# Splitting the memory-row hand-over and interleaving the Q and K passes in a recurrent memory transformer layer

## The chip, the cores and the metric

The kernel runs on one core of a Trainium2 chip. The metric is the device time of one execution in microseconds (us). Before the change, three runs took 2334.03, 2334.85 and 2330.82 us; their median is 2334.03 us. One more execution was profiled; its span from the first to the last instruction is 2335.8 us, at a mean granted TensorE clock of 0.98.

## The reference

Four layers in the order A, B, A, B work on `x` of 2048 tokens by 640 channels, each as `x = x + layer(layernorm(x))`. Layer A is a linear-memory attention over four segments; the change does not touch it. Layer B is recurrent over 64 segments of 32 tokens. Eight memory rows go in front of each segment, 32 heads of 128 channels attend over these 40 rows, and the output's first eight rows are the memory of the next segment:

```python
for s in range(n_seg):                       # 64
    xs = x[:, s * seg_len:(s + 1) * seg_len, :].copy()
    h = jnp.concatenate([mem, xs], axis=1)   # 8 + 32 rows
    q = jnp.einsum('btd,dhe->bhte', h, Wq)   # k and v likewise
    ...
    scores = jnp.where(mask[None, None], scores, -1000000000.0)
    p = _softmax(scores, axis=-1)
    o = jnp.einsum('bhqk,bhke->bhqe', p, v)
    o = jnp.einsum('bhte,hed->btd', o, Wo)
    mem = o[:, :M, :].copy()
    outs.append(o[:, M:, :])
```

A step can therefore not begin its projections of the memory rows before the output projection of the step before is complete.

## The kernel before, in words

**Order.** Every call on an engine goes through a recorder (line 85), which ties each instruction to the one before it on the same engine. So each engine's queue is the program order of the Python text, and nearly every instruction of the profile bears line 85; tiles (b_Qa, b_hT and so on) tell them apart. Waits between engines come from what reads and writes which tile.

**Layer B's step.** `layer_B` (line 661) runs 64 steps `s`; four of them make a tile `T` of 128 tokens, and `i4 = s % 4`. The stationary operand of a step, `hT[s]`, holds 5 chunks of 128 channels by 56 columns: 24 of the segment's own tokens, the 8 memory rows (columns 24 to 32), and 24 tokens of the next segment. The tokens are put there by GpSimd copies (`alloc_h`, line 729) one step ahead. A Q or K pass takes columns 24 to 56, so it computes the memory rows of this step and the tokens of the next; a V pass takes columns 0 to 32. The last 8 tokens of each segment, the tail, go another way: `tail_cols(T)` (line 776) gathers the tails of the four segments of a tile into `b_hx` on GpSimd, and `TailUnit`s project them for a whole tile at once.

**A pass.** `thin_parts` (line 750) makes five parts, one per chunk. Each part issues four matmuls into the four 32-partition strips of one PSUM tile (128x512 fp32). 32 heads need two passes each for Q, K and V; half b covers heads 16b to 16b+15. When a Q or K pass has run its last part (`QKPass.run`, line 1002), VectorE turns it by 32x32 blocks (`turn`, line 762, the STREAM_TRANSPOSE that writes b_TQ, two buffers), VectorE casts the memory rows into `QT[s]` or `KT[s]`, and GpSimd casts the other 24 columns into the tiles of step s+1 (`place`, line 768). When a V pass has ended, ScalarE (half 0) or VectorE (half 1) casts it into `b_Vsb`. The passes, the scores and the tail units take their PSUM tiles in turn from one pool of three (line 673).

**The order within a step** (lines 1097 to 1164): Q half 0, K half 0, Q half 1, two chunks of K half 1, scores of half 0, the other three chunks, V half 0 with the softmax sums of half 0 in it, scores of half 1, three chunks of V half 1, values of half 0, two chunks of V half 1, sums of half 1. `scores` (line 1022) begins with four mask matmuls that need neither Q nor K. Two ScalarE casts (`take`, line 1080) move the values of half 0 out of PSUM (b_OTL to b_OTsb). Then follow eight passes of two heads of the output projection (b_OPS), the values of half 1, and the last eight. `normalise` (line 1057) computes the inverse sums on ScalarE and multiplies b_PT on VectorE and on GpSimd.

**The hand-over.** After the output projection, VectorE turns all of b_OPS (128x320) into `b_TM` (line 1159), and two additions (line 1161) put the memory rows of all five chunks into `hT[s + 1]`. Meanwhile TensorE has filler: `fill` (line 956) takes from a queue of parts by written costs, about 0.44 us before the values of half 1, 0.66 us after them, and the rest behind the output projection. In steps with i4 of 1, 2 and 3 the queue holds the two tail units of V, Q or K of the next tile; in i4 = 0 it holds the deferred output projection of the tails of the last tile (b_OPSd). The last tile of a layer has no tail units. `flush` (line 822) finishes tail units whose parts are done: ScalarE casts V, VectorE turns Q and K and GpSimd casts them. Output rows are added to the residual on VectorE (b_XO, b_XOd): at once in steps with i4 = 1, in the middle of the next step otherwise.

Of the kernel before, what the change touches and what calls it, by code (L numbers as in the profile page):

```python
# [21 lines left out]
ALU = mybir.AluOpType  # L22
# [7 lines left out]
NCH = 5  # L30
# [630 lines left out]
def layer_B(nc, nc_raw, tc, C, W, br, outer, wo_src, x_src, xb_src, x_dst, general, nsteps=64, out_bf16=False):  # L661
# [3 lines left out]
    NT = nsteps // 4  # L665
    with ExitStack() as ctx:
# [34 lines left out]
        def ln_norm(g):  # L701
            xt = ln_x.pop(g)
            ln_n[g] = xt, layernorm_stats(nc, sm, C, xt[:], "b_ln")

        def ln_apply(g):
            xt, (mv, rstd) = ln_n[g]
            xn = ln_n[g] = wk.tile([128, D], BF16, name="b_xn", tag="xn")
            layernorm_apply(nc, xt[:], xn[:], mv, rstd)

        def ln_tr(g):  # L710
            xn = ln_n.pop(g)
            tps = pot.tile([128, NCH, 128], BF16, name="b_lntps", tag="ot")
            for c in range(NCH):
                nc.tensor.transpose(tps[:, c, :], xn[:, 128 * c:128 * c + 128], C.identb[:])
            xg = wk2.tile([128, NCH, 128], BF16, name="b_xnTg")
            nc.scalar.copy(xg[:], tps[:])
            xnT_g[g] = xg
# [6 lines left out]
        hT, QT, KT = {}, {}, {}  # L724
# [51 lines left out]
        def tail_cols(T):  # L776
            if T not in hx:
                hx[T] = wk.tile([128, NCH, 32], BF16, name="b_hx", tag="hx")
                v = xnT_g[T][:].rearrange("p c (i t) -> p c i t", t=32)[:, :, :, 24:32]
                nc.gpsimd.tensor_copy(hx[T][:].rearrange("p c (i t) -> p c i t", t=8), v)  # L780
            return lambda c: hx[T][:, c, :]
# [151 lines left out]
        for s in range(nsteps):  # L933
            last = (s == nsteps - 1)
            T, i4 = divmod(s, 4)
# [20 lines left out]
            def fill(us):  # L956

                while queue and us > 0.1:
                    cost, f = queue.pop(0)
                    f()  # L960
                    us -= cost
# [56 lines left out]
            def qk(Wt, name, b, dst):  # L1018

                QKPass(Wt, name, b, dst).run()  # L1020
# [27 lines left out]
            def sums(b):  # L1048

                sm_ = SP[b][:, 256:416].rearrange("p (r c) -> p r c", c=40)  # L1050
                for k in range(2):
                    for j in range(4):
                        nc.tensor.matmul(sm_[32 * j:32 * j + 32, :, 24 * k:40], lhsT=C.blk[:, j],
                                         rhs=PT[:, b, :, 0:16] if k else PT[:, b, :, 16:56], start=(k == 0), stop=(k == 1),
                                         tile_position=(0, 32 * j), skip_group_check=True)

            def normalise(b):

                R = (wk if general else sm).tile([128, 4, 40], F32, name="b_R", tag="R")
                flat = R[:].rearrange("p r c -> p (r c)")  # L1060
                nc.scalar.activation(out=flat, in_=SP[b][:, 256:416], func=ACT.Ln)
                nc.scalar.activation(out=flat, in_=flat, func=ACT.Exp, scale=-1.0)
                nc.vector.tensor_tensor(out=PT[:, b, :, 16:56], in0=PT[:, b, :, 16:56], in1=R[:], op=ALU.mult)
                nc.gpsimd.tensor_tensor(out=PT[:, b, :, 0:16], in0=PT[:, b, :, 0:16], in1=R[:, :, 24:40], op=ALU.mult)
                if not general:
                    nc.gpsimd.tensor_tensor(out=Rtot[:], in0=Rtot[:], in1=R[:], op=ALU.add)

            def values(b):
                for jp in range(2):
                    OTL[b, jp] = pair_tile("b_OTL")  # L1070
                for r in range(4):
                    for k in range(2):
                        V_ = Vtb[T] if k else Vsb
                        for j in range(4):
                            o = OTL[b, j // 2][:, j % 2, 40 * r + 24 * k:40 * r + 40]
                            nc.tensor.matmul(o, lhsT=V_[32 * j:32 * j + 32, b, 128 * r:128 * r + 128],
                                             rhs=PT[32 * j:32 * j + 32, b, r, 0:16] if k else PT[32 * j:32 * j + 32, b, r, 16:56],
                                             start=(k == 0), stop=(k == 1), tile_position=(32 * j, 0))

            def take(eng, b, jp):  # L1080
                h = 16 * b + 8 * jp
                evac(eng, OTsb[:, h:h + 8, :].rearrange("p (j r) c -> p j (r c)", j=2), OTL[b, jp][:, :, 0:160])
# [11 lines left out]
                    if not self.parts:  # L1094
                        evac(("act", "dve")[self.b], Vsb[:, self.b, :], self.ps[:])

            qk(W.wq, "b_Qa", 0, QT)
            qk(W.wk, "b_Ka", 0, KT)
            qk(W.wq, "b_Qb", 1, QT)
            if general:  # L1100
                row_max(0)
# [3 lines left out]
            K1.run(3)  # L1105
            while xn_pending:
                ln_tr(xn_pending.pop(0))
            if i4 == 0 and T + 1 < NT:
                tail_cols(T + 1)
            V0 = VPass(0)  # L1110
            V0.run(1)
            sums(0)
# [7 lines left out]
                nc.sync.dma_start(XO[32 * jj2:32 * jj2 + 24, :], x_src[32 * s:32 * s + 24, 320 * jj2:320 * jj2 + 320])  # L1120
            scores(1)
            V1 = VPass(1)
            V1.run(3)
            values(0)
            g_need = (s + 6) // 4 if s % 4 == 2 else NT
            if g_need < NT:
                ln_norm(g_need)
            V1.run(2)
            sums(1)
            take("act", 0, 0)  # L1130
            take("act", 0, 1)
            normalise(1)
            if g_need < NT:
                ln_apply(g_need)
                xn_pending.append(g_need)
            if i4 != 3:
                tails_to_seg(s + 1)
            op = OPass(lambda h: OTsb[:, h, 0:32], HORDER, "b_OPS", po, "op")
# [9 lines left out]
            ops = op.ps  # L1148
# [7 lines left out]
                deferred[T] = OPass(lambda h, t_=OTd: t_[:, h, :], HORDER, "b_OPSd")  # L1156
            if not last:
                TM = wk.tile([128, 10, 32], F32, name="b_TM", tag="TM")
                nc.vector.transpose(out=TM[:].rearrange("p g t -> p (g t)"), in_=ops[:])
                for hf in range(2):  # L1160
                    nc.vector.tensor_tensor(out=hT[s + 1][64 * hf:64 * hf + 64, :, 24:32], in0=TM[0:64, hf:10:2, 24:32],
                                            in1=TM[64:128, hf:10:2, 24:32], op=ALU.add)
            fill(9)
            flush()
            if not last and i4 == 3:
# [36 lines left out]
def full_kernel(tc, A_x, A_wq, A_wk, A_wv, A_wo, A_beta, B_x, B_mem0, B_Wq, B_Wk, B_Wv, B_Wo, B_seg_len, out, layers="ABAB"):  # L1202
    nc = tc.nc
    with ExitStack() as ctx:
# [14 lines left out]
        def run(general):  # L1219
            nc.scalar.preload_act_table_set("natural_log_exp_and_others")  # L1220
            nl = len(layers)
            assert layers == "AB" * (nl // 2)
            onc = _OrdNC(tc, nc, engines=ORDER_ENGINES)
            for li in range(0, nl, 2):
                lastl = (li == nl - 2)
                first = li == 0 and not general
                with ExitStack() as bridge, ExitStack() as outer:
                    outer.bridge = bridge
                    br = layer_A(onc, nc, tc, C, WA, A_wv, A_wo, xin if li == 0 else X, X, Xb, li == 0, general, outer, mem0,
                                 prep=prep if first else None, prefetch=loads if first else ())  # L1230
                    layer_B(onc, nc, tc, C, WB, br, outer, wo_src, X, Xb, xout if lastl else X, general, out_bf16=lastl)
# [61 lines left out]
```

## Time and profile before

| view | what it shows |
|---|---|
| span | 2335.8 us |
| busy, us | TensorE matmul 2225.5, VectorE 1576.3, GpSimd 1036.7, ScalarE 950.3 |
| layer B, typical step by i4 = 0, 1, 2, 3 | 12.92, 12.96, 13.06, 13.48 us from Q's first matmul to the next |
| VectorE, turning b_OPS | 126 times 517 ns |
| VectorE, additions into b_hT | 252 times 223 ns in the mean, 197 in the median |
| VectorE, turning a Q or K pass | 717 ns each |
| GpSimd, copy of tail columns into b_hx | 30 times 401 ns |

Busy time is the union of an engine's instruction times. Matmuls overlap, and their ends are modelled, so starts say more of TensorE than ends: the four matmuls of a chunk start within some 10 ns and the next four 216 ns after. In a list of waits, each row says which engine was idle, what ended that idle time, the total, how often and the longest. PEld is the loading of stationary operands, which runs ahead of the matmuls. In a timeline, each row has the start and the length in us, then the instructions merged into it; the bracket gives the idle time before and what ended it. POOL is GpSimd, DVE is VectorE, ACT is ScalarE.

### The profile page before, as it was taken

What the parts mean: (1) busy time and instruction counts of PE and PEld (TensorE: products, weight loads), DVE (VectorE), ACT (ScalarE), POOL (GpSimd) and SP (SyncE); (2) the same over time, 40 slices, a digit from 0 to 9 for tenths busy, and PEclk for the clock granted to TensorE, in tenths of its full rate; (3) what the DMA queues carried; (4) which work ended last, traced back from release to release, by engine and by line L of the source; (5) the groups of instructions that cost most, each with busy time, mean ns of one, the idle gap of its engine ahead of it and who ended that gap; (6) DMA issues with size and microseconds to landing.
All of it is one profiled execution on the core that took longest, in us unless ns stands there. A gap on an engine that the chain in (4) does not pass through costs nothing.

```text
span 2335.8 us, 122651 instructions
## 1 busy us (share of the span) xinstructions
PE 2225.5 (95%) x54988; PEld 1238.1 (53%) x54988; DVE 1576.3 (67%) x3618; ACT 950.3 (41%) x2207; POOL 1036.7 (44%) x2475
## 2 busy tenths in 40 slices
PE   6999989999999999999889899899999999999997
PEld 3444545555555555555545445455555555555554
DVE  5777746666666666666657777566666666666664
ACT  5776823323232333323257767223333233323332
POOL 3344534444444444444324445344444444444442
PEclk9999989999999999999989999999999999999998
DMA  6555540000000000000133334300000000000000
GB/s 165 146 148 152 161 142 20 21 18 20 18 19 19 20 21 20 21 15 17 31 104 115 108 117 127 124 18 15 17 15 17 16 18 16 17 18 16 14 12 14
DMA packets 90649, 123.38 MB, mean 53 GB/s; under 512 B 16496, under 2 KB 80000, under 8 KB 88192
## 3 DMA queue, kind: packets, MB, share of 16 engines
q1 hardware_dynamic: 87648, 111.84, 16.9%
q8 instruction: 431, 7.06, 1.3%
q10 hardware_dynamic: 2464, 3.61, 0.6%
q14 instruction: 106, 0.87, 0.1%
HBM read 89.17 MB, written 26.21 MB: 49 GB/s over the span
## 4 chain that ended last, share of the span: by engine, by line
PE 80%; DVE 10%; ACT 5%; issue 2%; DMA 2%; POOL 0%; SPq 0%; DVEq 0%; ACTq 0%; POOLq 0%
PE b_OPS L85 14%; PE b_V L85 13%; PE b_Qa L85 7%; PE b_tail L85 7%; PE b_Kb L85 6%; PE b_Ka L85 6%; PE b_Qb L85 6%; PE b_SP L85 4%; PE a_PP L85 4%; ACT a_PT L85 4%; PE b_OTL L85 3%; PE b_OPSd L85 3%; PE a_S L85 2%; PE a_pv L85 2%; DVE a_qk L85 2%
## 5 line engine op out<-in xcount | busy, mean ns | idle before, releaser
L85 PEld LDWEIGHTS <-b_hT 128*32 128x32 bf16 x15120 | 369.8, 96 | 334.7 <-DVE b_hT L85 66.6
L85 ACT ACTIVATE b_PT<-b_SP 128x224 bf16<-128x224 f32 x256 | 92.2, 360 | 784.6 <-DVE b_TQ L85 740.2
L85 PE MATMUL b_V<-b_wv,b_hT 128*32 128x512 bf16 x5040 | 355.8, 381 | 0.0
L85 ACT ACTIVATE a_PT<-a_S 128x768 bf16<-128x768 f32 (+1 forms) x384 | 326.7, 892 | 62.4 <-PE a_S L85 56.2
L85 PE MATMUL b_OPS<-b_wo,b_OTsb 128*32 128x320 bf16 x8192 | 329.9, 303 | 6.5 <-DVE b_OTsb L85 5.2
L85 PEld LDWEIGHTS <-b_OTsb 128*32 128x32 bf16 x8192 | 197.3, 97 | 115.4 <-DVE b_OTsb L85 49.4
L85 POOL CAST b_QT<-b_TQ 128x384 bf16<-128x384 f32 x254 | 142.7, 562 | 240.9 <-DVE b_TQ L85 240.9
L85 ACT CAST b_OTsb<-b_OTL 128x320 bf16<-128x320 f32 x384 | 151.0, 428 | 232.3 <-PE b_OTL L85 204.7
L85 POOL CAST b_KT<-b_TQ 128x384 bf16<-128x384 f32 x254 | 142.9, 563 | 175.5 <-DVE b_TQ L85 174.3
L85 POOL TENSOR_TENSOR b_PT<-b_PT,b_R 128x64 bf16<-128x64 bf16 x256 | 105.6, 412 | 222.1 <-ACT b_R L85 197.4
L85 POOL TENSOR_SCALAR_AFFINE_SELECT a_PT<-a_PT 128x256 bf16<-128x256 bf16 x256 | 109.0, 427 | 172.6 <-ACT a_PT L85 161.0
L85 PE MATMUL b_Kb<-b_wk,b_hT 128*32 128x512 bf16 x2520 | 182.5, 380 | 0.0
L85 PE MATMUL b_Qa<-b_wq,b_hT 128*32 128x512 bf16 x2520 | 162.3, 387 | 13.7 <-DVE b_hT L85 7.2
L85 PE MATMUL b_Ka<-b_wk,b_hT 128*32 128x512 bf16 x2520 | 160.0, 383 | 0.0
L85 PE MATMUL b_Qb<-b_wq,b_hT 128*32 128x512 bf16 x2520 | 158.1, 380 | 0.0
L85 PE MATMUL a_PP<-a_xnT,a_wt 128*128 128x512 bf16 x560 | 146.1, 394 | 5.2 <-DVE a_um L85 1.5
L85 DVE STREAM_TRANSPOSE b_TM<-b_OPS 128x320 f32<-128x320 f32 x126 | 65.1, 517 | 118.2 <-PE b_OPS L85 118.2
L85 PE MATMUL a_S<-a_qk 32*128 32x512 bf16 (+3 forms) x1024 | 137.3, 308 | 7.8 <-ACT a_PT L85 6.5
L85 DVE CAST b_Vsb<-b_V 128x512 bf16<-128x512 f32 x128 | 88.5, 692 | 74.6 <-PE b_SP L85 43.9
L85 DVE TENSOR_TENSOR b_PT<-b_PT,b_R 128x160 bf16<-128x160 bf16 x256 | 103.8, 405 | 48.3 <-ACT b_R L85 29.2
L85 DVE STREAM_TRANSPOSE b_TQ<-b_Qa 128x512 f32<-128x512 f32 x128 | 91.7, 717 | 65.7 <-PE b_Qa L85 45.4
L85 DVE CAST b_OTsb<-b_OTL 128x320 bf16<-128x320 f32 x128 | 62.9, 492 | 106.0 <-PE b_OTL L85 105.2
(165 smaller groups left out, 4270.0 us busy)
## 6 DMA issues: line engine op xcount, KB each, us to landing
a_wt<-a_wpad SPq DMA_DIRECT2D x112, 160.0 KB
b_XO<-xres SPq DMA_DIRECT2D x256, 30.0 KB
a_wvo<-in_A_wo_dram SPq DMA_DIRECT2D x8, 800.0 KB
b_wq<-in_B_Wq_dram SPq DMA_DIRECT2D x20, 256.0 KB
b_wk<-in_B_Wk_dram SPq DMA_DIRECT2D x20, 256.0 KB
xres<-a_xo SPq DMA_DIRECT2D x16, 320.0 KB
xres_bf<-a_xb SPq DMA_DIRECT2D x32, 160.0 KB
b_wv<-in_B_Wv_dram SPq DMA_DIRECT2D x20, 256.0 KB
```

Of the source, the lines that this page charges most:

```text
L85: r = f(*a, **k)
```

## The change

The edits are all in layer B's step:

- The Q and K passes of half 0 are made together. Two chunks of Q, two of K, three of Q, three of K take the place of five and five.
- The copy of the next tile's tail columns (`tail_cols(T + 1)`, in steps with i4 = 0) moves from behind the K passes to behind `normalise(1)`.
- V half 1 runs two chunks ahead of the values of half 0 and three after them, where it ran three and two.
- b_OPS is turned in two parts, chunks 0 and 1 and then chunks 2 to 4 (128 and 192 columns), each followed by its two additions.

```diff
-            qk(W.wq, "b_Qa", 0, QT)
-            qk(W.wk, "b_Ka", 0, KT)
+            Q0, K0 = QKPass(W.wq, "b_Qa", 0, QT), QKPass(W.wk, "b_Ka", 0, KT)
+            Q0.run(2)
+            K0.run(2)
+            Q0.run(3)
+            K0.run(3)
             qk(W.wq, "b_Qb", 1, QT)
...
-            if i4 == 0 and T + 1 < NT:
-                tail_cols(T + 1)
             V0 = VPass(0)
...
             V1 = VPass(1)
-            V1.run(3)
+            V1.run(2)
             values(0)
             g_need = (s + 6) // 4 if s % 4 == 2 else NT
             if g_need < NT:
                 ln_norm(g_need)
-            V1.run(2)
+            V1.run(3)
             sums(1)
             take("act", 0, 0)
             take("act", 0, 1)
             normalise(1)
+            if i4 == 0 and T + 1 < NT:
+                tail_cols(T + 1)
...
-                nc.vector.transpose(out=TM[:].rearrange("p g t -> p (g t)"), in_=ops[:])
-                for hf in range(2):
-                    nc.vector.tensor_tensor(out=hT[s + 1][64 * hf:64 * hf + 64, :, 24:32], in0=TM[0:64, hf:10:2, 24:32],
-                                            in1=TM[64:128, hf:10:2, 24:32], op=ALU.add)
+                for c0, c1 in ((0, 2), (2, NCH)):
+                    nc.vector.transpose(out=TM[:, 2 * c0:2 * c1].rearrange("p g t -> p (g t)"), in_=ops[:, 64 * c0:64 * c1])
+                    for hf in range(2):
+                        nc.vector.tensor_tensor(out=hT[s + 1][64 * hf:64 * hf + 64, c0:c1, 24:32], in0=TM[0:64, 2 * c0 + hf:2 * c1:2, 24:32],
+                                                in1=TM[64:128, 2 * c0 + hf:2 * c1:2, 24:32], op=ALU.add)
```

## The prediction

> **What bounds the kernel now.** I read the page's busy shares and the shares of the chain of work that ended last, then the waits of all engines, then the timeline of single steps of layer B.
>
> ```profile
> PE 2225.5 (95%) x54988; PEld 1238.1 (53%) x54988; DVE 1576.3 (67%) x3618; ACT 950.3 (41%) x2207; POOL 1036.7 (44%) x2475
> ...
> PE 80%; DVE 10%; ACT 5%; issue 2%; DMA 2%; POOL 0%; SPq 0%; DVEq 0%; ACTq 0%; POOLq 0%
> ```
> TensorE is the bound: 95% busy, 80% of the chain. An edit that adds no matmul can only remove or add gaps between them. The waits name the gaps (total us, times, longest):
> ```profile
> PEld L85 <- DVE b_hT L85: 66.6, 126, 1.7
> PEld L85 <- ACT b_Vsb L85: 53.9, 127, 0.4
> ```
> 126 is the number of step boundaries. PEld idles ahead of its matmuls without harm, so I price gaps from matmul starts. Passes that never wait follow each other at 1.08 us per 20 matmuls (0.216 per weight chunk of four, last start to next start 0.206). The boundary at 612.48, after a step with i4=1 (start, us, what):
> ```profile
> 611.22 1.25 PE L85 MATMUL b_tail<-b_wv,b_hx 128*32 128x512 bf16 x20
> 611.45 0.52 DVE L85 STREAM_TRANSPOSE b_TM<-b_OPS 128x320 f32<-128x320 f32 x1 [1.38 <-PE b_OPS L85]
> 612.00 0.43 DVE L85 TENSOR_TENSOR b_hT<-b_TM 64x40 bf16<-64x40 f32 x2
> ...
> 612.48 0.98 PEld L85 LDWEIGHTS <-b_hT 128*32 128x32 bf16 x24 [0.50 <-DVE b_hT L85]
> ```
> The filler could hand over at 611.22+1.08 = 612.30; Q starts at 612.48, 0.05 after the second addition: 0.18 lost. One boundary later (i4=2):
> ```profile
> 624.40 0.52 DVE L85 STREAM_TRANSPOSE b_TM<-b_OPS 128x320 f32<-128x320 f32 x1 [0.44 <-PE b_OPS L85]
> ...
> 624.81 0.40 POOL L85 COPY b_OTdef<-b_OTsb 128x256 bf16<-128x256 bf16 x1
> 624.95 0.54 DVE L85 TENSOR_TENSOR b_hT<-b_TM 64x40 bf16<-64x40 f32 x2
> ```
> Here the additions take 0.54, not 0.43: the first meets POOL's OTdef copy. Loss 0.28, and the same at i4=3. After i4=0 (deferred filler) it is 0.035. A second place, in the step at 704.46:
> ```profile
> 705.85 0.72 DVE L85 STREAM_TRANSPOSE b_TQ<-b_Qa 128x512 f32<-128x512 f32 x1 [0.19 <-PE b_Qa L85]
> ...
> 706.93 0.72 DVE L85 STREAM_TRANSPOSE b_TQ<-b_Ka 128x512 f32<-128x512 f32 x1
> ...
> 707.68 0.23 DVE L85 CAST b_KT<-b_TQ 128x128 bf16<-128x128 f32 x1
> ...
> 708.21 0.19 PE L85 MATMUL b_SP<-b_QT,b_KT 128*32 128x40 bf16 x4
> ```
> Scores of half 0 use KT 0.30 after its cast ended; a wake-up costs 0.05, so the slack is 0.25. A third:
> ```profile
> 710.50 0.59 ACT L85 CAST b_Vsb<-b_V 128x512 bf16<-128x512 f32 x1 [0.16 <-PE b_V L85]
> ...
> 710.64 0.84 PE L85 MATMUL b_V<-b_wv,b_hT 128*32 128x512 bf16 x12
> ...
> 711.41 0.20 PE L85 MATMUL b_OTL<-b_PT,b_Vsb 32*128 32x40 bf16 x4
> ...
> 711.94 0.75 ACT L85 CAST b_OTsb<-b_OTL 128x320 bf16<-128x320 f32 x2 [0.51 <-PE b_OTL L85]
> ...
> 712.41 1.27 PE L85 MATMUL b_OPS<-b_wo,b_OTsb 128*32 128x320 bf16 x32
> ```
> OPS begins 0.05 after the first OTsb cast, 0.17 to 0.19 after the last sums matmul started; sums before a V pass shows 0.02. So some 0.165 is lost in each step.
>
> [...] the addition takes 0.30 behind OTdef and 0.196 alone; POOL's b_PT multiplication takes 0.45 when DVE's began 0.04 earlier, 0.30 alone. [...] Here a 1-element scaling takes 0.154 and the 40-element addition 0.196.
>
> **Part 1, memory rows in two parts.** STREAM_TRANSPOSE takes 0.517 for 320 elements and 0.717 for 512: 1.04 ns an element plus 0.184. So 128 elements are estimated at 0.317 and 192 at 0.384. From 0.154 and 0.196, additions of 16 and 24 elements are 0.17 and 0.18. With 0.034 between DVE instructions, the first part is ready 0.317+2x(0.034+0.17) = 0.73 after TM's start (before: 0.98), the second 0.84 later. DVE gains 0.6 of work per boundary.
> - After i4=1, Q could start at 0.73+0.05 = 0.78, but the filler ends at 0.855: full gain, 0.18.
> - After i4=2 and 3, OTdef starts 0.40 after TM and the new first addition at 0.35. [...] the second addition waits: the copy lets go some 0.145 before its end (0.80), so 0.655+0.17 = 0.83, Q at 0.88, gain 1.135-0.88 = 0.255. Bounds: [...] 0.28 if nothing collides. I take 0.255.
> - After i4=0, 0.035.
>
> The second part must come within the 16 matmuls of chunks 0 and 1 of Q and K, 0.864 (0.875 with the first chunk): it needs 0.84. After i4=1, 0.09 is to spare, after i4=2 and 3 0.03. I cost it at nothing.
>
> **Part 2, interleaving.** Q ends after 28 matmuls instead of 20: 0.43 later. Its transposition moves from 1.386 to 1.82 after Q's start; K's ends no later on TensorE but queues behind it: 1.82+0.717+0.034+0.226+0.034+0.717+0.034+0.226 = 3.81, awake at 3.86. The scores need KT at 3.75: 0.107 lost in each step. What DVE has ahead is done by 1.82: deferred-output additions by 1.62, stores of i4=1 by 1.76, the tail unit's transposition by 1.54. After i4=3, two hT copies follow on POOL (from 1.70 and 1.93 now; behind the later tail cast about 2.51 and 2.74), and Q's cast [...] asks at 2.57: about 0.085 more. Bounds for the wait: nothing (were DVE quicker) to 0.2. The three accumulators turn in the same order; tail 1 is free by 1.54 and wanted at 2.17, K by 3.55 and wanted at 3.68.
>
> **Part 3, two V1 chunks before the values.** They start 0.24 earlier (8 matmuls plus the 0.312 that the change of tiling takes): 6.71 after Q's start instead of 6.95. They need V0's ACT cast, done at 6.62, awake at 6.67; in i4=3 it is 7.18 against 7.15, 0.03 lost. The ACT casts of OTL then come 0.24 sooner and OPS follows the sums at once: 0.165 gained, 0.14 in i4=3. V1 ends when it did, so its DVE cast (7.92) stays.
>
> **Part 4, tail copy.** POOL's b_hx copy (0.40) makes the b_PT product of i4=0 end at 6.89 instead of 6.61, too late for values at 6.71; moved behind half 1's product it is hidden, for its first reader is the next step's filler. It is queued ahead of the QTt copy, c_tot and OTdef; OTdef waits for the deferred pass anyway. No DMA moves. Nothing by itself.
>
> **Sum** for four steps, wait at the start counted in the step it delays: i4=0 0.035+0.165-0.19 = 0.01; i4=1 0.18+0.17-0.11 = 0.24; i4=2 0.255+0.17-0.11 = 0.32; i4=3 0.255+0.14-0.11 = 0.285; 0.855 together. Times 15 tiles 12.8, less 0.25 for the first two steps, which wait for weights; the last tile, whose two boundaries without filler gain the full 0.25, adds 0.7. 13.25 a layer, **26.5 us** for both. The profiled span is 2335.8, the unprofiled median 2334.0 (2330.8 to 2334.9): 2334.0-26.5 = **2307.5**.
>
> **Rivals.**
> - [...] 0.2 less at 60 boundaries, 12: 2320. For it: the margin is 0.05. Against: DVE won with 0.04.
> - Delays add up: the second part is 0.05 late and KT 0.1 later than reckoned, at 126 steps some 17: 2325. For it: slacks of 0.03 and durations interpolated. Against: rows of this trace give them.
> - KT doesn't wait, as DVE is quicker than the sum: 126 x 0.107 = 13 more: 2294. Against: every term is measured.
> - **Slower:** the change doesn't do what it says. If readers of hT wait for all writes to the tile, Q starts after the second part, at 1.62 instead of 1.03: 0.59 more at 126 boundaries, 74, less 19 from part 3, plus 15 from KT: 2404. It decides once Q's start passes 1.03+0.165-0.12 = 1.08 after TM. Against: OPS at 712.41 reads OTsb while the second cast into it (to 712.69) still runs, so waits go by region.
>
> **Numbers.** Forecast 50%, port 21%, delays 12%, no KT wait 9%, slower 8% (with lesser causes). A measurement here tells 0.2% (4.7 us) from no change. Faster, below 2329.4: the forecast, the port case, no KT wait and two thirds of the delays case, 88%; within 0.2%: the rest of the delays and one of the slower eight, 5%; slower 7%. The range 2297 to 2327 holds the forecast, its bounds, the port case and most of the delays case; it leaves out no KT wait and slower, 17%.
>
> **What would show it.** Q starting 0.78 to 0.88 after TM; b_QT's first cast 0.43 later relative to Q, and a new wait of scores on b_KT of 0.1; OPS 0.16 sooner; the waits on b_hT smaller. A Q start beyond 1.08 after TM, a K chunk 2 that waits, or values held by b_Vsb in most steps would make it wrong.

## The result and the profile after

The changed kernel took a median of 2304.09 us (four runs, 2297.37 to 2307.99) beside 2333.35 us for the kernel before (four runs, 2330.82 to 2334.85): 29.3 us less, a ratio of 0.987 with a 95% interval of 0.985 to 0.990. In a later comparison (e9 below) it took 2298.68 beside 2333.8, a ratio of 0.986 (0.983 to 0.988). The forecast was 2307.5 with a range of 2297 to 2327. The profiled execution has a span of 2300.8 us at a mean granted clock of 0.98, 35.0 less than the one before.

The busy shares and the chain that ended last, on the page after:

```profile
PE 2195.3 (95%) x54988; PEld 1234.9 (54%) x54988; DVE 1623.6 (71%) x3996; ACT 961.6 (42%) x2207; POOL 1028.5 (45%) x2475
...
PE 81%; DVE 8%; ACT 5%; issue 3%; DMA 2%; SPq 1%; POOL 0%; DVEq 0%; ACTq 0%; POOLq 0%
...
L85 DVE STREAM_TRANSPOSE b_TM<-b_OPS 128x128 f32<-128x128 f32 x252 | 88.2, 350 | 123.6 <-PE b_OPS L85 119.7
```

TensorE makes the same 54988 matmuls and is still the bound. VectorE makes 378 instructions more (126 boundaries, one transposition and two additions more at each) and works 47.3 us longer; its share of the chain falls from 10 to 8%. The transposition of b_OPS is now 252 instructions; 350 ns is the mean of its two sizes.

The total of waits hides what happened (who waited for whom, total us, times, longest):

```profile
PEld L85 <- issue: 225.3, 739, 3.1
PEld L85 <- DVE b_hT L85: 69.2, 218, 1.4
PEld L85 <- ACT b_Vsb L85: 52.8, 128, 0.4
PEld L85 <- DVE b_KT L85: 35.5, 221, 0.2
```

The wait on b_hT was 66.6 us at 126 boundaries and is now 69.2 in 218 pieces, and the one on b_KT rose from 16.0 (100 times) to 35.5. Read as a bill, this says that nothing was gained and K's wait was added. But these are idle times of the weight load, which runs ahead; an earlier weight load can idle longer without delaying a matmul. Of the 218 pieces, 96 with 36.5 us in all stand at Q's start, where all 66.6 stood before, and 122 with 32.7 us stand before chunk 2, where the matmuls of a typical step start no later for it (below). The starts of matmuls tell what was gained. The typical step (lower quartile by i4 of the steps with filler, 116 in all; us from Q's first matmul to the next):

| step | before | after | gained | forecast |
|---|---|---|---|---|
| i4 = 0 | 12.92 | 12.775 | 0.145 | 0.01 |
| i4 = 1 | 12.96 | 12.594 | 0.36 | 0.24 |
| i4 = 2 | 13.06 | 12.619 | 0.44 | 0.32 |
| i4 = 3 | 13.48 | 13.073 | 0.41 | 0.285 |
| four steps | 52.42 | 51.06 | 1.36 | 0.855 |

So the typical step gained more than forecast. Over the 116 steps that is 39.8 us, and the forecast's terms give 0.855 x 29 = 24.8. The 116 steps as they ran gained 32.7: 7.1 went to steps that are longer than typical. All 126 steps together went from 1672.2 to 1637.4 us, so of the 35.0 only 0.2 lies outside them. In the profile of the later comparison (e9) these steps take 1637.4 us again, though its span is 4.5 us shorter (2296.3): what lies outside the steps, above all layer A, which no edit touches, takes 658.9 to 664.1 us in the profiles of this document. A difference of some 5 us between two runs can therefore come from there.

The boundary after a step with i4 = 1, from the timeline after (start, length, instructions):

```profile
602.94 1.25 PE L85 MATMUL b_tail<-b_wv,b_hx 128*32 128x512 bf16 x20
603.16 0.32 DVE L85 STREAM_TRANSPOSE b_TM<-b_OPS 128x128 f32<-128x128 f32 x1 [1.38 <-PE b_OPS L85]
603.52 0.38 DVE L85 TENSOR_TENSOR b_hT<-b_TM 64x16 bf16<-64x16 f32 x2
603.92 0.38 DVE L85 STREAM_TRANSPOSE b_TM<-b_OPS 128x192 f32<-128x192 f32 x1
...
604.02 0.61 PE L85 MATMUL b_Qa<-b_wq,b_hT 128*32 128x512 bf16 x8
604.34 0.39 DVE L85 TENSOR_TENSOR b_hT<-b_TM 64x24 bf16<-64x24 f32 x2
...
604.88 0.39 PE L85 MATMUL b_Qa<-b_wq,b_hT 128*32 128x512 bf16 x4
```

Q starts 0.86 after the turn of b_OPS, just behind the filler, and before the second part has been added. The second part is complete at 604.73, and its first reader, chunk 2 of Q, starts at 604.88 = 604.02 + 0.86, as if there were no hand-over. The second place, at Q's and K's turns of the next step:

```profile
616.64 0.62 PE L85 MATMUL b_Qa<-b_wq,b_hT 128*32 128x512 bf16 x8
...
618.46 0.72 DVE L85 STREAM_TRANSPOSE b_TQ<-b_Qa 128x512 f32<-128x512 f32 x1 [0.28 <-PE b_Qa L85]
...
619.21 0.23 DVE L85 CAST b_QT<-b_TQ 128x128 bf16<-128x128 f32 x1
619.35 0.71 DVE L85 STREAM_TRANSPOSE b_TQ<-b_Ka 128x512 f32<-128x512 f32 x1
620.09 0.23 DVE L85 CAST b_KT<-b_TQ 128x128 bf16<-128x128 f32 x1
...
620.39 0.19 PE L85 MATMUL b_SP<-b_QT,b_KT 128*32 128x40 bf16 x4
```

Q's turn begins at 1.82, as forecast. Then look at the cast of Q: it is reported until 619.44, and the turn of K begins at 619.35, 0.09 earlier. K's cast ends at 3.68 instead of 3.81, and the scores start at 3.75, which is when TensorE comes to them anyway.

### The profile page after: what moved, and what is told of

Its sections match the earlier page's. It is cut to its first block, busy times and chain, and to the rows that moved or that the text cites. A ratio compares the mean times of both kernels' runs of the same rounds, so it can differ in the third digit from the quotient of the medians.

```text
span 2300.8 us, 123029 instructions
## 1 busy us (share of the span) xinstructions
PE 2195.3 (95%) x54988; PEld 1234.9 (54%) x54988; DVE 1623.6 (71%) x3996; ACT 961.6 (42%) x2207; POOL 1028.5 (45%) x2475
## 4 chain that ended last, share of the span: by engine, by line
PE 81%; DVE 8%; ACT 5%; issue 3%; DMA 2%; SPq 1%; POOL 0%; DVEq 0%; ACTq 0%; POOLq 0%
PE b_V L85 13%; PE b_OPS L85 12%; PE b_tail L85 10%; PE b_Qa L85 6%; PE b_Kb L85 6%; PE b_Ka L85 6%; PE b_Qb L85 6%; PE b_SP L85 5%; PE a_PP L85 4%; ACT a_PT L85 4%; PE b_OTL L85 3%; PE b_OPSd L85 3%; PE a_S L85 2%; PE a_pv L85 2%; DVE a_qk L85 1%
## 5 line engine op out<-in xcount | busy, mean ns | idle before, releaser
L85 PEld LDWEIGHTS <-b_hT 128*32 128x32 bf16 x15120 | 372.3, 96 | 311.3 <-DVE b_hT L85 69.2
L85 PE MATMUL b_Qa<-b_wq,b_hT 128*32 128x512 bf16 x2520 | 183.2, 384 | 5.0 <-DVE b_hT L85 5.0
L85 PE MATMUL b_Ka<-b_wk,b_hT 128*32 128x512 bf16 x2520 | 182.2, 382 | 0.0
L85 DVE STREAM_TRANSPOSE b_TM<-b_OPS 128x128 f32<-128x128 f32 x252 | 88.2, 350 | 123.6 <-PE b_OPS L85 119.7
L85 POOL TENSOR_TENSOR b_Rtot<-b_Rtot,b_R 128x160 bf16<-128x160 bf16 x256 | 126.6, 494 | 0.0
```

Source lines behind the costliest of these rows:

```text
L85: r = f(*a, **k)
```

## The experiments

Two theories stood against each other from the typical steps. **Theory A**: K's wait is next to nothing, because VectorE's cast of Q and turn of K overlap (0.09 above), so what the hand-over brings is kept. **Theory B**: K's wait is there as forecast, and the surplus comes from the values. None of the twelve kernels changes what is computed. Each was compared with the kernel before on the same chip.

### The parts alone (e1 to e4)

**e1**: split and interleaving; the values and the tail copy stay as before (this diff and the next ones are against the changed kernel, if not said otherwise).

```diff
+            if i4 == 0 and T + 1 < NT:
+                tail_cols(T + 1)
             V0 = VPass(0)
...
-            V1.run(2)
+            V1.run(3)
             values(0)
...
-            V1.run(3)
+            V1.run(2)
...
             normalise(1)
-            if i4 == 0 and T + 1 < NT:
-                tail_cols(T + 1)
```

> Hand-over in two parts and Q/K interleaved, values and tail copy as before. Theory A (VectorE starts an instruction that needs no wait before the one ahead has ended, so K is turned sooner than the prediction's sum and the scores wait only after steps with i4 = 3, 0.05 us): boundary gains 0.035, 0.18, 0.255, 0.255 less 0.05, some 0.67 us in four steps, 21 us in all: about 2312 to 2315, and scores of half 0 with no wait on b_KT in most steps. Theory B (the prediction's term holds, K's wait costs 0.107 to 0.19 a step, and what was gained beyond the forecast comes from the values): 0.22 in four steps, 7 us: about 2326.

**e2**: the other half of the change: the kernel before with the values and the tail copy moved (diff against the kernel before; the tail copy moves as in the change).

```diff
-            V1.run(3)
+            V1.run(2)
             values(0)
...
-            V1.run(2)
+            V1.run(3)
...
```

> Two V1 chunks before the values and the tail copy moved, hand-over and passes as before. Theory A: OPS starts 0.165 us sooner in three steps of four and 0.14 in the fourth, 0.635 in four steps, 20 us: about 2313. Theory B: this part carries most of the measured 29 us: about 2306 to 2308, OPS 0.23 sooner or more.

**e3**: the kernel before with the Q and K passes interleaved, nothing else.

```diff
-            qk(W.wq, "b_Qa", 0, QT)
-            qk(W.wk, "b_Ka", 0, KT)
+            Q0, K0 = QKPass(W.wq, "b_Qa", 0, QT), QKPass(W.wk, "b_Ka", 0, KT)
+            Q0.run(2)
+            K0.run(2)
+            Q0.run(3)
+            K0.run(3)
```

> Only the Q and K passes of half 0 interleaved; the rows come in one part. Theory A: Q is turned 0.43 us later, but K is ready at 3.74 after Q's start and wanted at 3.75: no wait, no change, 2331 to 2336. Theory B: K at 3.86, 0.107 lost in each of 126 steps: about 2347.

**e4**: the kernel before with b_OPS turned in two parts, nothing else.

```diff
-                nc.vector.transpose(out=TM[:].rearrange("p g t -> p (g t)"), in_=ops[:])
...
+                for c0, c1 in ((0, 2), (2, NCH)):
+                    nc.vector.transpose(out=TM[:, 2 * c0:2 * c1].rearrange("p g t -> p (g t)"), in_=ops[:, 64 * c0:64 * c1])
...
```

> Only the rows turned in two parts; Q runs its five chunks in a row as before, so its third chunk is wanted 0.44 us after its start and the second part comes 0.84 after the first. Both theories: Q starts 0.78 to 1.0 us after the turn instead of 1.03 to 1.13 but stands before chunk 2 until 1.62 (1.72 after i4 = 2 and 3), so it ends 0.145 later than before: 126 x 0.145 = 18, about 2352. If waits went by whole tiles, Q would not start before 1.62 at all: about 2408.

Measured, beside 2335.54 us for the kernel before (19 runs):

| kernel | median us (range, runs) | ratio (95%) | typical step i4 = 0, 1, 2, 3 |
|---|---|---|---|
| before | 2335.54 (2330.99 to 2341.92, 19) | 1 | 12.92 12.96 13.06 13.48 |
| e1 split and interleaving | 2316.13 (2307.45 to 2318.53, 6) | 0.9914 (0.9899 to 0.9929) | 12.94 12.77 12.80 13.23 |
| e2 values and tail copy | 2317.62 (2315.89 to 2322.65, 6) | 0.9929 (0.9917 to 0.9941) | 12.75 12.78 12.885 13.33 |
| e3 interleaving alone | 2335.41 (2329.13 to 2339.04, 14) | 0.9999 (0.9988 to 1.0009) | 12.92 12.96 13.06 13.48 |
| e4 split alone | 2358.38 (2353.03 to 2360.34, 4) | 1.0097 (1.0082 to 1.0113) | 13.29 13.15 13.15 13.64 |

What follows:

- e3 decides between the theories. Interleaving alone costs the typical step nothing, though Q is turned 0.43 later; the forecast's wait of 0.107 at each of 126 steps would have been 13 us. K's cast ends 3.68 after Q's start there too.
- e2's typical steps gain 0.17 or 0.18 (0.15 in i4 = 3) where the forecast has 0.165 and 0.14, so next to no surplus comes from the values, and Theory B is out.
- The parts add up: in four typical steps e1 gains 0.68 and e2 0.675; the whole gains 1.36. In time, e1 gains 19.4 and e2 17.9, together 37, and the whole 29 and 35 in its two comparisons.
- e4 shows that the two parts of the change need each other. The split alone is slower by 22.8 us (18 were expected), because chunk 2 of Q then comes after 8 matmuls and not after 16.

This is e4's boundary after a step with i4 = 0 (timeline):

```profile
595.86 0.32 DVE L85 STREAM_TRANSPOSE b_TM<-b_OPS 128x128 f32<-128x128 f32 x1 [1.38 <-PE b_OPS L85]
...
596.62 0.38 DVE L85 STREAM_TRANSPOSE b_TM<-b_OPS 128x192 f32<-128x192 f32 x1
...
596.85 0.60 PE L85 MATMUL b_Qa<-b_wq,b_hT 128*32 128x512 bf16 x8
597.03 0.57 DVE L85 TENSOR_TENSOR b_hT<-b_TM 64x24 bf16<-64x24 f32 x2
597.17 0.40 POOL L85 COPY b_OTdef<-b_OTsb 128x256 bf16<-128x256 bf16 x1 [2.93 <-PE b_OPSd L85]
...
597.65 0.83 PE L85 MATMUL b_Qa<-b_wq,b_hT 128*32 128x512 bf16 x12 [0.20 <-DVE b_hT L85]
```

Eight matmuls of Q run from 596.85, while the second part is only being turned: in this kernel waits go by region of b_hT, and the slower rival (readers wait for the whole tile) is refuted. The other twelve wait until 597.65, 0.37 after the first eight's 0.43 of work is done. Here the second pair of additions also takes 0.57 instead of 0.39, since GpSimd's b_OTdef copy begins between the two. This second pair meets the copy only after i4 = 0 (step 13.29, 0.37 longer, against 0.09 to 0.19 in the others). At 30 steps the 0.23 above the expected 0.145 are 7 us, so this alone puts the result above the 18 us that I had expected. The change has this meeting too, but there the second part is not wanted so early.

### The tail copy (e5, e10)

**e5**: the changed kernel with the tail copy in its old place. **e10** is the same kernel on another chip, beside the change itself (e9).

```diff
+            if i4 == 0 and T + 1 < NT:
+                tail_cols(T + 1)
             V0 = VPass(0)
...
             normalise(1)
-            if i4 == 0 and T + 1 < NT:
-                tail_cols(T + 1)
```

> The changed kernel with the tail copy where it was. Theory A: in steps with i4 = 0 GpSimd's product for half 0 ends behind the copy, at 6.95 us after Q's start, where the values begin at 6.79; their memory-tail matmuls wait until 7.0, 0.18 lost in 30 steps, 5 us: about 2309. Rival: the product isn't wanted so early, or the wait is made up before OPS: 2304, no change.

> The changed kernel with the tail copy where it was, once more. Theory A (its 0.18 us in the step of i4 = 0 counts, and the 2299.7 of the first measurement came from fewer irregular stalls): 5 us above the changed kernel of this call. Rival (what is lost in that step is given back elsewhere): within 2 us of it.

e5 took 2299.72 us (2296.86 to 2301.38, four runs) beside 2332.28, a ratio of 0.9859 (0.9837 to 0.9881): by time it missed the expectation of some 2309 and is no slower than the change. By the step it met it: i4 = 0 takes 12.953 instead of 12.775. The place, in e5's timeline:

```profile
581.86 0.41 POOL L85 COPY b_hx<-b_xnTg 128x160 bf16<-128x160 bf16 x1
...
582.24 0.30 POOL L85 TENSOR_TENSOR b_PT<-b_PT,b_R 128x64 bf16<-128x64 bf16 x1
...
582.38 0.20 PE L85 MATMUL b_OTL<-b_PT,b_Vsb 32*128 32x40 bf16 x4
...
582.59 0.19 PE L85 MATMUL b_OTL<-b_PT,b_Vtb 32*128 32x16 bf16 x4
```

GpSimd's product of b_PT stands behind the copy and ends at 582.54; the values that read it start 0.21 after their neighbours, where 0.04 is usual (610.75 and 610.79 in the changed kernel). That 0.18 at 30 steps is 5 us. In time, e10 took 2303.42 us (2302.57 to 2306.45), a ratio of 0.9871 (0.9848 to 0.9893), beside e9's 2298.68: 4.7 more, but the intervals overlap. The profiles do not show that the move shortens the whole. Over the 116 steps, e5 and e10 take 1491.1 and 1492.0 us, the change and e9 take 1490.9 and 1491.9: what a typical step loses with the copy in its old place, fewer long steps give back (below; 6.0 and 6.7 us of them, beside 10.4 and 11.5). And of the 5.7 us between the profiled spans of e10 and e9, 4.0 lie outside the 126 steps, where the two kernels are the same. So the loss in the typical step is shown, but no gain in time from moving the copy.

### K's turn, and the additions beside the copy (e6, e7)

**e6**: in the changed kernel, Q's cast of half 0 is made twice, which puts one more VectorE instruction between Q's turn and K's cast.

```diff
                         place("dve", tq, self.b, heads(self.dst[s]), 0, 8, 24)
+                        if self.b == 0 and self.dst is QT:
+                            place("dve", tq, self.b, heads(self.dst[s]), 0, 8, 24)
```

> The changed kernel with VectorE's cast of Q half 0 issued twice, which puts one more 0.23 us instruction between the turns of Q and K. Theory A (the turn of K has no slack left): with the overlap of neighbours the cast costs 0.14 to 0.2, K's wait 0.12 to 0.2 in each of 126 steps, 15 to 25 us: 2319 to 2329. Rival (K's turn has slack, the sum of the prediction was wrong in kind): 2304 to 2308.

It took 2346.07 us (2341.32 to 2348.73, four runs) beside 2332.28, a ratio of 1.0064 (1.0043 to 1.0086): 42 more than the change's 2304, where 15 to 25 had been expected. The direction fits Theory A, the size does not. Its timeline shows why:

```profile
611.07 0.72 DVE L85 STREAM_TRANSPOSE b_TQ<-b_Qa 128x512 f32<-128x512 f32 x1
...
611.82 0.67 DVE L85 CAST b_QT<-b_TQ 128x128 bf16<-128x128 f32 x2
611.85 0.56 POOL L85 CAST b_QT<-b_TQ 128x384 bf16<-128x384 f32 x1 [3.83 <-DVE b_TQ L85]
612.40 0.70 DVE L85 STREAM_TRANSPOSE b_TQ<-b_Ka 128x512 f32<-128x512 f32 x1
...
613.14 0.23 DVE L85 CAST b_KT<-b_TQ 128x128 bf16<-128x128 f32 x1
...
613.42 0.10 PEld L85 LDWEIGHTS <-b_KT 128*32 128x32 bf16 x4 [0.16 <-DVE b_KT L85]
```

The two casts take 0.67, not 2 x 0.23: GpSimd's cast of Q begins at 611.85, before the second, and ends at 612.41; the second is reported until 612.49. K's cast ends 4.11 after Q's start instead of 3.68, and a typical step grows by 0.26 to 0.43, over 1.5 in four steps. Once more the turn of K begins before the casts' reported end (612.40 against 612.49). So K's cast does bound the scores as soon as it comes later than about 3.7; in the change it stands on the edge of that, and the slack of 0.25 that it had before is used up.

**e7**: the changed kernel with chunks 0 to 2 in the first part and 3 and 4 in the second.

```diff
-                for c0, c1 in ((0, 2), (2, NCH)):
+                for c0, c1 in ((0, 3), (3, NCH)):
```

> The changed kernel with the rows turned as chunks 0 to 2 and 3 to 4 (192 and 128 columns); the passes as changed. Theory A [...]: the first addition asks 0.42 after the turn's start, behind OTdef's copy (0.40), so after i4 = 2 and 3 both additions come after it and Q starts 1.10 after the turn instead of 0.88: 60 times 0.22, 13 us, about 2317. Rival (the copy and the addition share, the order doesn't matter): Q at 0.86 to 0.88, 2303 to 2305.

It took 2308.29 us (2306.88 to 2309.61, four runs) beside 2332.28, a ratio of 0.99 (0.9879 to 0.9921), where 2317 was expected. The boundary after i4 = 2:

```profile
616.79 0.38 DVE L85 STREAM_TRANSPOSE b_TM<-b_OPS 128x192 f32<-128x192 f32 x1 [0.45 <-PE b_OPS L85]
...
617.19 0.40 POOL L85 COPY b_OTdef<-b_OTsb 128x256 bf16<-128x256 bf16 x1
617.21 0.63 DVE L85 TENSOR_TENSOR b_hT<-b_TM 64x24 bf16<-64x24 f32 x2
...
617.89 0.62 PE L85 MATMUL b_Qa<-b_wq,b_hT 128*32 128x512 bf16 x8
```

The copy begins 0.02 before the first addition and now holds it (0.41 instead of 0.18): 0.63 for two additions that take 0.39 alone, and Q starts 1.10 after the turn instead of 0.88. This is the rival put at 2320 (the prediction's "port case"): after i4 = 2 and 3 GpSimd's copy begins ahead of the first addition, here because the transposition has 64 columns more. Typical steps of i4 = 2 and 3 lose 0.225 and 0.22, as expected; the steps of i4 = 0 gain 0.06, which was not expected: there Q's cast takes 0.23 again, so it no longer meets the hT copies. Over the 116 steps the typical steps lose some 12 us and the steps as they ran 8.3, since fewer of them are long. In time, e7 is 4.2 us above the change's first median and 9.6 above its second, so by time alone the loss isn't clear.

### Taking what is left (e8, e9, e11, e12)

Two losses are left at i4 = 0: TensorE is idle between the deferred filler and the second half of the output projection, and the two hT copies on GpSimd hold Q's cast (0.30 instead of 0.23; K's cast ends at 3.75). **e8** raises the filler behind the values and puts these copies behind the K pass. **e11** does the first alone, **e12** the second alone, **e9** is the change once more.

```diff
-                alloc_h(s + 1)
...
             K0.run(3)
+            if not last:
+                alloc_h(s + 1)
...
-            fill(0.66)
+            fill(0.75)
```

> The changed kernel with 0.75 in place of 0.66 in the second fill (one more part of the deferred pass ahead of OPS in steps with i4 = 0, nothing else) and GpSimd's two hT copies for the next step moved behind the K pass of half 0. Theory A: OPSd to OPS has 0.16 idle in i4 = 0, of which a part of 0.136 fills most: 30 times 0.13, 4 us; the copies no longer hold Q's cast after i4 = 3: 30 times 0.05, 1.5 us: about 2298.5. Rival (what is filled there is missing at the hand-over): 2302 to 2304.

> The changed kernel once more, beside the next three on one chip. Both theories: 2298 to 2306; the typical step of i4 = 0 is 12.78 us.

> The changed kernel with 0.75 in place of 0.66 in the second fill alone. Theory A: step of i4 = 0 shorter by 0.135, 12.645; 4 us below the changed kernel of this call. Rival (the gain of the combined kernel came from the copies): no difference.

> The changed kernel with GpSimd's hT copies behind the K pass of half 0 alone. Theory A [...]: step of i4 = 0 shorter by 0.055, and K cast by 3.68; 1.5 us below the changed kernel of this call, within what the runs can tell. Rival: the combined kernel's gain comes from here: 5 us or more.

| kernel | median us (range, runs) | ratio (95%) | typical step i4 = 0 |
|---|---|---|---|
| e8 both | 2293.75 (2290.42 to 2299.01, 5) | 0.9842 (0.982 to 0.9863) | 12.585 |
| e9 the change again | 2298.68 (2296.64 to 2305.09, 4) | 0.9855 (0.983 to 0.988) | 12.771 |
| e11 more filler | 2299.57 (2294.41 to 2303.44, 5) | 0.9848 (0.9826 to 0.987) | 12.638 |
| e12 copies later | 2301.04 (2298.51 to 2302.87, 4) | 0.9857 (0.9835 to 0.988) | 12.720 |

e8 ran beside 2332.28, the other three beside 2333.8. In the step of i4 = 0 the two edits do what they should, 0.133 and 0.051 beside e9, and add up to e8's 0.186. From the last deferred matmul to the second half of the output projection it is 0.13 (e11) and 0.15 (e8) instead of 0.29, and K's cast ends at 3.68 with the copies moved.

But the rival was right in part: more filler has a price at the hand-over. With one part less left behind the output projection, the b_OTdef copy starts 1.17 after the turn of b_OPS instead of 1.31, and meets the additions of the second part. One such boundary of e8:

```profile
537.06 0.60 PE L85 MATMUL b_Qa<-b_wq,b_hT 128*32 128x512 bf16 x8
537.38 0.40 POOL L85 COPY b_OTdef<-b_OTsb 128x256 bf16<-128x256 bf16 x1 [2.46 <-DVE b_TM L85]
537.38 0.64 DVE L85 TENSOR_TENSOR b_hT<-b_TM 64x24 bf16<-64x24 f32 x2
...
538.08 0.83 PE L85 MATMUL b_Qa<-b_wq,b_hT 128*32 128x512 bf16 x12
```

Chunk 2 of Q starts 1.02 after Q's start instead of 0.86. In e8 it is late by over 0.03 in 16 of 28 steps with i4 = 1, in e11 in 6, in the change in 3. Even where it is not late, Q's turn behind the additions starts 0.05 later, and the typical step of i4 = 1 is 12.635 in e8 and e11 instead of 12.59. This takes back a third of the 0.133. In the time, e11 and e12 cannot be told from the change: what is left would be some 3 us, and the profiled runs lost 12.6 and 13.1 us to long steps, beside 11.5 for e9. e8 is the fastest kernel of the study and faster than the kernel before beyond doubt; against the change its interval overlaps, so that it beats the change is shown for four typical steps (0.15 less) and not for the time.

### The long steps, left open

A step counts as long where it exceeds the typical step of its i4 by over 0.05 us. In the profiled runs the excess is, in us (and steps so counted), with the tail copy in its old place: before 3.5 (18), e3 3.0 (16), e4 3.4 (20), e1 5.8 (25), e5 6.0 (22), e10 6.7 (32); with the tail copy moved: e7 7.5 (29), e6 7.8 (32), e2 8.1 (36), the change 10.4 (38), e8 11.4 (43), e9 11.5 (41), e11 12.6 (42), e12 13.1 (41). All profiles with the copy moved have more than all without, one profile for each kernel. In i4 = 2 the typical step isn't even the usual one: 16 of 30 steps are long in the change, 7 before. Most of the excess lies at the values of half 1. One, in the change's timeline:

```profile
690.39 0.09 PEld L85 LDWEIGHTS <-b_Vsb 32*128 32x128 bf16 x1 [0.26 <-DVE b_PT L85]
...
690.97 0.20 PE L85 MATMUL b_OTL<-b_PT,b_Vsb 32*128 32x40 bf16 x4 [0.51 <-issue]
690.97 0.10 PEld L85 LDWEIGHTS <-b_Vsb 32*128 32x128 bf16 x3 [0.49 <-issue]
```

One of four weight loads is made at 690.39, then nothing until 690.97, and "issue" says that no wait of the trace explains it. Elsewhere the cause can be seen: at 1645.12 a residual addition on VectorE waited 0.97 for its row from memory, and Q's turn behind it was 0.9 late; but there are only five such waits, 2.4 us together.

The traces do say where TensorE stops with nothing to wait for. The page after lists a DMA queue of the kind "instruction" (packets, MB, share of the DMA engines):

```profile
q8 instruction: 431, 7.06, 1.3%
```

Its 431 packets are of equal size (16.4 KB), one for every 255 of the 109976 matmuls and weight loads. Call it a stall where a matmul comes over 0.1 us later behind the one before it than the same matmul does in the median step of its i4. Counted along the matmuls and weight loads in blocks of 256, all nine stalls of the profile before, other than those at Q or the scores, lie at the same place of a block. In the change 28 stalls, 7.3 us together, lie at that place, and TensorE goes on 1.24 to 1.60 us after the end of a packet of this queue. It never passes the place sooner than 1.24 us after a packet's end, in 347 passes; at the median place of a block, 27% of the passes come within 1.2 us. From this I take it that TensorE stood there for its next instructions, but that is not shown: no run was made to test it. Why the stalls are more frequent with the tail copy moved stays open.

## Why the prediction was right, and what was off

- **Hand-over (part 1): right.** The transpositions take 0.317 and 0.383 (estimated 0.317 and 0.384), the additions 0.171 and 0.179 (0.17 and 0.18). From the filler's last matmul to Q it is 0.206 instead of 0.385 after i4 = 1, 0.23 instead of 0.49 after i4 = 2 and 3, and 0.126 instead of 0.161 after i4 = 0: gains of 0.18, 0.26 and 0.035 against 0.18, 0.255 and 0.035. The meeting with the b_OTdef copy after i4 = 2 and 3 went as reckoned: the first addition begins 0.05 ahead of the copy, and the second is held and takes 0.27 instead of 0.17. That the first would go ahead unhindered was an estimate; e7 shows the other order and its price of 0.22. The second part cost nothing in a typical step, as said. One meeting was overlooked: after i4 = 0 the second part's additions meet the b_OTdef copy (0.35 for the last one instead of 0.18), so that the additions into b_XOd, which were to be done by 1.62, end at 1.79, just ahead of Q's turn at 1.82. e8 shows what follows when they come later.
- **Interleaving (part 2): the term that was mis-sized.** The sum to 3.81 put 0.034 between the end of Q's cast and the turn of K. It is -0.085: K's turn starts before the cast's reported end, K's cast ends at 3.68, and the scores wait about nothing, not 0.107. After i4 = 3 it ends at 3.75 and costs 0.055, not 0.19. In four steps that is 0.47 of the 0.505 by which the typical steps beat the sum. The rival in which KT does not wait, given 9%, was the true one at this place, though its 2294 was not reached; e3 shows it, and e6 shows how near the edge is.
- The sum took every gap between VectorE instructions as 0.034, from pairs in which the second needs the first's result and from the two additions into b_hT. The trace of before had the answer. The pair itself overlaps there where VectorE is behind, in the first step of layer B:

```profile
318.55 0.23 DVE L85 CAST b_QT<-b_TQ 128x128 bf16<-128x128 f32 x1
318.69 0.71 DVE L85 STREAM_TRANSPOSE b_TQ<-b_Ka 128x512 f32<-128x512 f32 x1
```

  And in steps with i4 of 0 to 2, VectorE's product of b_PT, reported until 6.44 us after Q's start, is followed at 6.37 by an instruction that does not need it, BATCH_NORM_STATS2 or an addition to b_XO.
- **Values (part 3): right.** In e2, which has this part without the hand-over, the output projection starts 0.157 to 0.167 sooner (0.165 forecast), 0.143 in i4 = 3 (0.14). From V's last matmul (128*32) to the first of the values (32*128) it is 0.312 in the median, before and after.
- **Tail copy (part 4): right as "nothing by itself"**: left in place it would have cost 0.18 in each typical step of i4 = 0 (e5, e10), though the 116 steps together would have been no longer.
- **Long steps: not foreseen.** They took back 7 us of the 15 by which the typical steps beat the sum. So the forecast of 2307.5 came within 3.4 of the first median and 8.8 of the second partly by luck: two misses have opposite signs.

## What to carry to other kernels

Before a sum of instruction times decides, look in the trace for a pair of the same kind: here the gap was -0.085 for K's turn behind Q's cast, which it does not need, and 0.03 for an instruction that reads the result of the one before, but also between the two additions into b_hT, which do not need each other. This hand-over could be split to advantage only because its reader got work on the first part to fill the time of the second: the split alone cost 23 us here and the interleaving alone nothing, and together they gained 19. Price a gap from the starts of matmuls, since the wait totals of a weight load that runs ahead rose here while the time fell.

## What the runs showed of the hardware

- VectorE's next instruction can start before the reported end of the one before. In the change, K's turn starts 0.079 to 0.087 before the end of Q's cast (126 steps), and an addition to b_XO 0.077 before the end of the product of b_PT (94 times, median). It is not so for every pair that could overlap: the second addition into b_hT starts 0.034 after the end of the first (252 times), and the transposition behind the second addition 0.031 after its end (126 times; 603.90 and 603.92 above). Where the second reads what the first wrote, as Q's cast behind Q's turn, the gap is 0.034 (128 times). No run was made to tell what decides between the two.
- An addition into b_hT that begins while GpSimd's b_OTdef copy runs takes longer: 0.301 instead of 0.196 before (59 times), 0.268 instead of 0.172 (60) and 0.353 instead of 0.180 (29) in the change, in the median. The copy takes 0.40 throughout. If the last part of such an addition, as long as one takes alone, is the addition itself, it begins 0.14 before the copy's reported end, in all three groups. The first addition, which in the change begins 0.048 ahead of the copy (median of 60), takes its usual 0.171 in 51 of the 60; in e7 the copy began 0.02 ahead and the first addition took 0.41. So a few hundredths of a microsecond decide the order, and that was worth 0.22 a boundary.
- GpSimd's product of b_PT takes 0.45 where VectorE's product began 0.047 earlier (median of 106 before), and 0.304 beside VectorE's additions to b_XO (28 times before): this is the 0.30 that the prediction calls "alone". What it is that holds one engine while the other works was not tested.
